# A hand-ordered pipeline for linear attention followed by a token and channel MLP: the next batch's attention between MLP matmuls, full 512-token groups, crossbar turns

## The chip, the cores and the metric

The kernel runs on one core of one Trainium2 chip. A core has a matmul engine (PE), which reads weights and moving operands from the on-chip buffer (SBUF) and writes accumulators (PSUM); a vector engine (DVE), a scalar engine (ACT) and a general engine (POOL); a queue engine (SyncE, SP in the profile); and 16 DMA engines that all queues share. Each engine runs its own instructions in order and waits on semaphores for the others.

The metric is the device time of one execution in microseconds. Every run is timed beside runs of the kernel before on the same chip. A ratio in this document is the mean time of one kernel's fast runs over the mean time of the other's fast runs of the same rounds, so it is not quite the ratio of the medians that stand beside it. A profile shows the span from the first to the last instruction, which is 1.7 to 1.9 us shorter than the time where both are on record for one execution.

## The reference, cut to what matters

```python
# q, k, v: 8 batches, 8 heads, 576 tokens, 64 channels, float32
def phi(x, c, s):                       # c, s: cos and sin of the token's position
    r = np.maximum(x, 0.0)
    return np.concatenate([r * c, r * s], axis=-1)        # 128 features
kv  = einsum('bhsf,bhsd->bhfd', phi(k), v);   z = phi(k).sum(tokens)
num = einsum('bhsf,bhfd->bhsd', phi(q), kv)
den = einsum('bhsf,bhf->bhs',  phi(q), z) + 1e-06
x   = (num / den) as [batch, 576 tokens, 512 channels]

h   = relu(x.T @ w_tok1) @ w_tok2       # mixes tokens: 576 -> 256 -> 576
u   = x + h.T
out = u + relu(u @ w_ch1) @ w_ch2       # mixes channels: 512 -> 1536 -> 512
```

About four fifths of the arithmetic, counted from these shapes, is in the last line, the channel MLP. Each batch's channel MLP needs its u, and u needs the batch's attention and both token products first. Batches do not depend on each other.

## The kernel before

It handles one batch after another; a scheduler orders each engine's instructions. 576 tokens are four tiles of 128 and one of 64. In this document, to *turn* a tile is to transpose it, to *evict* is to copy a finished result from PSUM to SBUF, *features* are the products phi(q) and phi(k), and *token-1* and *token-2* are the products with `w_tok1` and `w_tok2`. `uT` is the turned u, the input of the channel MLP.

```python
    for b in range(B):
        for ci, (o, sz) in enumerate(s_sizes):                # 128, 128, 128, 128, 64 tokens
            nc.sync.dma_start(out=qt[:sz], in_=q[b, :, o:o + sz, :].rearrange("h s d -> s h d"))
            nc.sync.dma_start(out=kt[:sz], in_=k[b, :, o:o + sz, :].rearrange("h s d -> s h d"))
            nc.gpsimd.dma_start(out=vt[:sz], in_=v[b, ...])   # cast to bf16 on the way
            # ... features: relu(q)*cos and *sin on ACT, relu(k)*cos and *sin on DVE ...
            for h in range(H):
                nc.tensor.matmul(kv_ps[:F, h * D:(h + 1) * D], kph, vt[:sz, h, :], ...)
                nc.tensor.matmul(z_ps[:F, h:h + 1], kph, ones[:sz, :], ...)      # one column
            for g in range(2):                                # turn the q features on PE
                for hh in range(HH):
                    nc.tensor.transpose(tr_ps[:F, hh, :sz], qph, ident[:sz, :sz])
                nc.scalar.copy(qpT[...], tr_ps[:F, :, :sz])
        # ... kv and z to SBUF ...
        for ci, (o, sz) in enumerate(s_sizes):
            for h in range(H):
                nc.tensor.matmul(num_ps[:sz, h * D:(h + 1) * D], lw, kv_sb[...], ...)
                nc.tensor.matmul(den_ps[:sz, h:h + 1], lw, z_sb[:F, h:h + 1], ...)
            # ... x_sb = num / den on DVE ...
        # ... b1_ps: 2 x 5 matmuls with w_tok1, relu on ACT; u_ps: 5 x 2 with w_tok2; u = u_ps + x ...
        for ci, (o, sz) in enumerate(s_sizes):                # turn u on PE, in float32
            for cj in range(NCC):
                nc.tensor.transpose(t_ps[...], u_sb[...], ident_f[:sz, :sz])
            nc.scalar.copy(uT[:, :, o:o + sz], t_ps[:, :, :sz])
        for mi in range(NCH):                                 # 12 slices of 128 hidden channels
            for (no, nsz) in [(0, 512), (512, 64)]:
                for ki in range(NCC):
                    nc.tensor.matmul(c_ps[:, no:no + nsz], w_ch1[...], uT[:, ki, no:no + nsz], ...)
            # ... relu to h1T, on ACT and DVE in turn ...
        for ci, (o, sz) in enumerate(s_sizes):                # five outputs, the last of 64 tokens
            for ki in range(NCH):
                nc.tensor.matmul(o_ps[:sz, :], h1T[:, ki, o:o + sz], w_ch2[:, ki, :], ...)
            # ... add u, store ...
```

## Time and profile before

| | kernel before |
|---|---|
| time, median of 2 runs | 418.03 us (417.87 to 418.19) |
| span of the profile | 415.3 us |
| first channel-MLP matmul | 69.2 us |
| one batch: channel MLP / the rest | about 25.2 / about 20.5 us |
| busy: PE, DVE, ACT, POOL | 85%, 39%, 39%, 15% |

The page of the profiled execution gives, for each engine, the busy time, its share of the span and the number of instructions; then slices of the span with the busy tenths; then shares of the chain that ended last.

```profile
span 415.3 us, 7475 instructions
...
PE 352.4 (85%) x3168; PEld 201.4 (48%) x3168; DVE 161.3 (39%) x332; ACT 162.6 (39%) x283; POOL 62.7 (15%) x72
...
PEclk9999559998799989998999979998999899998999
DMA  9999983029901393029702791029402900110002
...
PE 76%; DMA 7%; SPq 6%; DVE 5%; ACT 5%; issue 1%; DVEq 0%; ACTq 0%
...
```

PE is busy 85% of the span, yet its clock as granted by the throttle (PEclk, tenths) keeps dropping, and the DMA engines are at eight or nine tenths for the first six slices. Where does PE's time go? The windows view of two stretches, first one batch without its channel MLP and then its channel MLP, answers. Its columns are the stretch, its length, busy time and instruction count of PE, of PE's weight loads, of DVE, ACT and POOL, the granted clock, the DMA share and GB/s.

```profile
...
140.70:161.00 20.30, 18.47 (x242) 12.56 (x242) 12.75 (x31) 16.00 (x29) 6.72 (x5) 0.92 1.11 154
161.00:186.00 25.00, 25.00 (x156) 11.99 (x154) 7.31 (x10) 4.01 (x7) 0.00 (x0) 1.00 0.12 43
...
```

In the first of these two, attention and token mixing, PE counts as busy for 18.5 of 20.3 us at clock 0.92. The timeline of that stretch shows what this busy time is (start, length, engine, line, operation, shapes, count; in brackets the idle time before and what ended it).

```profile
...
146.94 0.24 PE L156 MATMUL den_ps<-z_sb,qpT 128*128 128x1 bf16 x4 [0.53 <-DVE den_sb L159]
...
150.42 3.41 PE L171 MATMUL b_ps<-x_sb,w_tok_118 128*128 128x512 bf16 x10
153.76 1.23 PE L133 MATMUL z_ps<-ones,kp 128*128 128x1 bf16 x40
...
157.73 2.82 PE L187 MATMUL t_ps<-ident_f,u_sb 128*128 128x128 f32 x20
160.88 0.38 PE L197 MATMUL c_ps<-uT,w_ch_127 128*128 128x512 bf16 x1 [0.33 <-ACT uT L189]
```

Ten token-1 matmuls take 3.41 us here, against 12 matmuls of the same width in 2.59 us in the MLP (216 ns each). The attention stretch of the batch before, 94 to 115 us, has a mean clock of 0.84. PE also waits for DVE or ACT several times, for 0.3 to 0.5 us each. Then 40 one-column z matmuls (1.2 us) and 20 turns of u in float32 (2.8 us) stand in the chain. Nothing of the next batch's MLP can fill these gaps, because its u does not exist yet.

### The profile page before, as it was taken

The numbers are of one execution on the slowest core, as the hardware profiler recorded it, in microseconds if no ns is written. First come the engines' busy times: TensorE is split into PE (matmuls) and PEld (weight loads), VectorE is DVE, ScalarE is ACT, GpSimd is POOL, SyncE is SP. The second block draws the span as 40 slices with busy tenths as digits, with TensorE's granted clock in tenths as the row PEclk, the third lists the DMA queues.
The fourth block names the chain that finished last, engine by engine and source line by source line (L and its number), as shares of the span: only waits on it lengthen the run. The fifth ranks groups of instructions, "written<-read, shape, count | busy, mean of one in ns | idle before, by whom it ended". The sixth has DMA issues, their size and how long they took to land.

```text
span 415.3 us, 7475 instructions
## 1 busy us (share of the span) xinstructions
PE 352.4 (85%) x3168; PEld 201.4 (48%) x3168; DVE 161.3 (39%) x332; ACT 162.6 (39%) x283; POOL 62.7 (15%) x72
## 2 busy tenths in 40 slices
PE   0005178998999999998999899998999899999996
PEld 0004154547454555447554655456554755465542
DVE  2002253327422554328332653346332743326231
ACT  4115164208531384209630664128520873051410
POOL 7363000006000320006000600024000600000000
PEclk9999559998799989998999979998999899998999
DMA  9999983029901393029702791029402900110002
GB/s 183 205 192 182 169 151 77 2 86 156 161 2 42 98 187 76 0 103 169 130 2 76 137 165 25 25 91 196 91 0 86 85 5 0 52 65 0 2 25 90
DMA packets 121043, 37.26 MB, mean 90 GB/s; under 512 B 113521, under 2 KB 115889, under 8 KB 121009
## 3 DMA queue, kind: packets, MB, share of 16 engines
q1 hardware_dynamic: 80256, 28.32, 30.7%
q0 software_dynamic: 40752, 8.46, 23.0%
q8 instruction: 25, 0.41, 0.5%
q14 instruction: 10, 0.07, 0.1%
HBM read 35.78 MB, written 9.44 MB: 109 GB/s over the span
## 4 chain that ended last, share of the span: by engine, by line
PE 76%; DMA 7%; SPq 6%; DVE 5%; ACT 5%; issue 1%; DVEq 0%; ACTq 0%
PE c_ps L197 23%; DMA kt<-in_k_dram 7%; PE b_ps L171 6%; PE num_ps L154 4%; PE tr_ps L141 4%; PE u_ps L179 4%; ACT uT L189 3%; SPq L113 3%; PE kv_ps L131 3%; SPq L112 3%; PE t_ps L187 3%; PE den_ps L156 2%; PE z_ps L133 2%; DVE kp L124 2%; DVE u_sb L181 1%; DVE kp L122 1%
## 5 line engine op out<-in xcount | busy, mean ns | idle before, releaser
L197 PE MATMUL c_ps<-uT,w_ch_127 128*128 128x512 bf16 (+1 forms) x768 | 97.0, 286 | 2.6 <-ACT uT L189 2.6
L114 POOL DMA_DIRECT2D vt<-in_v_dram x40 | 49.2, 1242 | 257.1 <-PE tr_ps L141 247.3
L142 ACT COPY qpT<-tr_ps 128x512 bf16<-128x512 bf16 (+1 forms) x80 | 40.4, 544 | 111.8 <-PE tr_ps L141 111.1
L197 PEld LDWEIGHTS <-w_ch_127 128*128 128x128 bf16 x768 | 51.0, 97 | 48.8 <-issue 2.5
L210 PEld LDWEIGHTS <-h1T 128*128 128x128 bf16 (+1 forms) x480 | 46.9, 100 | 55.3 <-issue 3.4
L205 DVE TENSOR_SCALAR h1T<-c_ps 128x576 bf16<-128x576 f32 x48 | 36.4, 758 | 83.2 <-PE c_ps L197 83.2
L203 ACT ACTIVATE h1T<-c_ps 128x576 bf16<-128x576 f32 x48 | 31.2, 650 | 61.4 <-PE c_ps L197 60.4
L120 ACT ACTIVATE qp<-qt,bias_112,cos_t 128x512 bf16<-128x512 f32 (+1 forms) x40 | 32.2, 805 | 23.1 <-DMA qt<-in_q_dram 23.1
L133 PE MATMUL z_ps<-ones,kp 128*128 128x1 bf16 (+1 forms) x320 | 10.5, 164 | 34.5 <-DVE kp L124 28.1
L181 DVE TENSOR_TENSOR u_sb<-u_ps,x_sb 128x512 f32<-128x512 f32 (+1 forms) x40 | 24.6, 681 | 30.0 <-PE u_ps L179 30.0
L122 DVE TENSOR_SCALAR kp<-kt,cos_t 128x512 bf16<-128x512 f32 (+1 forms) x40 | 19.9, 498 | 39.9 <-DMA kt<-in_k_dram 35.6
L156 PE MATMUL den_ps<-z_sb,qpT 128*128 128x1 bf16 (+1 forms) x320 | 18.5, 169 | 18.0 <-DVE den_sb L159 15.8
L121 ACT ACTIVATE qp<-qt,bias_112,sin_t 128x512 bf16<-128x512 f32 (+1 forms) x40 | 32.2, 804 | 1.7 <-DMA qt<-in_q_dram 1.7
L141 PE MATMUL tr_ps<-ident,qp 128*128 128x128 bf16 (+1 forms) x320 | 30.4, 221 | 0.7
L189 ACT CAST uT<-t_ps 128x512 bf16<-128x512 f32 (+1 forms) x40 | 20.1, 548 | 21.1 <-PE t_ps L187 20.1
L133 PEld LDWEIGHTS <-kp 128*128 128x128 bf16 (+1 forms) x320 | 9.4, 96 | 37.8 <-DVE kp L124 28.4
L164 DVE TENSOR_TENSOR x_sb<-num_ps,den_sb 128x512 bf16<-128x512 f32 (+1 forms) x40 | 25.3, 683 | 5.6 <-PE num_ps L154 4.9
L171 PE MATMUL b_ps<-x_sb,w_tok_118 128*128 128x512 bf16 (+1 forms) x80 | 26.7, 486 | 0.0
L156 PEld LDWEIGHTS <-qpT 128*128 128x128 bf16 (+1 forms) x320 | 16.0, 104 | 21.1 <-issue 17.9
L124 DVE TENSOR_SCALAR kp<-kt,sin_t 128x512 bf16<-128x512 f32 (+1 forms) x40 | 21.4, 535 | 3.3 <-DMA kt<-in_k_dram 3.3
L187 PE MATMUL t_ps<-ident_f,u_sb 128*128 128x128 f32 (+1 forms) x160 | 21.8, 273 | 0.9
L141 PEld LDWEIGHTS <-qp 128*128 128x128 bf16 (+1 forms) x320 | 20.8, 100 | 3.3 <-issue 0.2
(127 smaller groups left out, 307.3 us busy)
## 6 DMA issues: line engine op xcount, KB each, us to landing
qt<-in_q_dram SPq DMA_DIRECT2D x32, 256.0 KB, 6.5
kt<-in_k_dram SPq DMA_DIRECT2D x32, 256.0 KB, 5.5
out_dram<-res SPq DMA_DIRECT2D x32, 256.0 KB, 2.0
vt<-in_v_dram POOLq DMA_DIRECT2D x32, 128.0 KB, 6.9
w_ch_127<-in_moe_w_ch_dram POOLq DMA_DIRECT2D x4, 384.0 KB, 10.0
w_ch_132<-in_moe_w_ch_dram POOLq DMA_DIRECT2D x12, 128.0 KB, 8.4
qt<-in_q_dram SPq DMA_DIRECT2D x8, 128.0 KB, 3.9
kt<-in_k_dram SPq DMA_DIRECT2D x8, 128.0 KB, 3.5
```

What stands on the lines that cost most here:

```text
L114: nc.gpsimd.dma_start(out=vt[:sz], in_=v[b, :, o:o + sz, :].rearrange("h s d -> s h d"))
L120: nc.scalar.activation(qp[:sz, :, 0, :], qt[:sz], AF.Relu, bias=bias0[:sz], scale=c_s)
L121: nc.scalar.activation(qp[:sz, :, 1, :], qt[:sz], AF.Relu, bias=bias0[:sz], scale=s_s)
L141: nc.tensor.transpose(tr_ps[:F, hh, :sz], qph, ident[:sz, :sz])
L142: nc.scalar.copy(qpT[:F, g * HH:(g + 1) * HH, o:o + sz], tr_ps[:F, :, :sz])
L156: nc.tensor.matmul(den_ps[:sz, h:h + 1], lw, z_sb[:F, h:h + 1], start=True, stop=True)
L171: nc.tensor.matmul(b1_ps, w_tok1[:sz, ci, mi * P:(mi + 1) * P], x_sb[:sz, ci, :], start=(ci == 0), stop=(ci == NSC - 1))
L187: nc.tensor.transpose(t_ps[:P, cj, :sz], u_sb[:sz, ci, cj * P:(cj + 1) * P], ident_f[:sz, :sz])
L189: nc.scalar.copy(uT[:, :, o:o + sz], t_ps[:, :, :sz])
L197: nc.tensor.matmul(c_ps[:, no:no + nsz], w_ch1[:, ki, mi * P:(mi + 1) * P], uT[:, ki, no:no + nsz], start=(ki == 0), stop=(ki == NCC - 1))
L205: nc.vector.tensor_relu(h1T[:, mi, :], c_ps)
L210: nc.tensor.matmul(o_ps[:sz, :], h1T[:, ki, o:o + sz], w_ch2[:, ki, :], start=(ki == 0), stop=(ki == NCH - 1))
```

## The change

The intent: PE should never run attention alone. Every instruction is placed by hand. While PE does the channel MLP of group g, the attention steps of batch g+1 are put between its matmuls, one small step after every four MLP matmuls, and the features of batch g+2 are computed on ACT, DVE and POOL. Further parts of the same change:

- Each batch's MLP takes 512 of its 576 tokens; the eight tails of 64 tokens form a ninth group at the end, so every MLP matmul has 512 columns.
- z and den become a 65th column of the kv and num matmuls.
- The q features and u are turned by crossbar DMA transposes from the SyncE queue instead of on PE. Only the first batches' turns stay on PE.
- Tokens are dealt to partitions so that four or five neighbouring tokens are contiguous in HBM: packets of 1 to 1.25 KB instead of 256 bytes, two loads per tensor and batch.

```diff
-    for b in range(B):
-        ... loads, features, kv, z, turns, num, den, token mixing, turns, MLP of batch b ...
+    ctx.enter_context(tc.manual_schedule())
+    ... batch 0 up to its uT, and the features and q turns of batch 1 ...
+    for g in range(B + 1):                       # nine groups; the last holds the tails
+        b = g + 1                                # attention of this batch now
+        f = g + 2                                # features of this one
+        if g + 3 < B:
+            loads(g + 3, (nc.sync, nc.sync))
+        for s in range(24):
+            if s < 12: ps = mlp1(g, s)           # four matmuls of 512 columns
+            else:      mlp2(g, t, part, mps[t])  # four matmuls of 512 columns
+            if b < B:
+                if s < 5:          kv(b, s);  if s == 4: kv_out(b, ACT)
+                elif 6 <= s < 11:  num(b, s - 6); x_out(b, s - 6)
+                elif s in (12, 13): b1(b, s - 12); b1_out(b, s - 12, ACT)
+                elif s in (15, 16):
+                    u_mm(b, s - 15); u_out(b, s - 15)
+                    u_cast(b, s - 15, ACT); uturn_dma(b, s - 15)
+                elif s == 17 and b % 2: tail_mm(b); tail_out(b)
+            ... evict mlp1 or mlp2 of this step ...
+            if f < B:
+                if 7 <= s < 12:    kfeat(f, s - 7, DVE, ACT); vcast(f, s - 7, POOL)
+                if 13 <= s < 23 and s % 2 == 1:
+                    qfeat(f, j, DVE, ACT); qturn_dma(f, j)
 ... (cut: helpers, the new layout of weights and tokens, the start)
+    def uturn_dma(b, c):
+        nc.sync.dma_start_transpose(out=uT[b % 2][...], in_=u_bf[...])     # 256 KB
+    def qturn_dma(b, j):
+        nc.sync.dma_start_transpose(out=qpT[:, :, j, :], in_=qp[j]...)     # 256 KB
```

(Engine names are written out here; `s`, `j`, `t` and `part` are counters. The part before the loop is the *start* in what follows, and the change from one group to the next is a *boundary*.)

## The prediction

> **What bounds it now.** The chain of waits gives PE 76% of the 415.3 us span. The timeline splits it: first channel-MLP matmul at 69.2 us; then each batch takes 45 to 46.5 us: about 25.2 of channel MLP at granted clock 1.00, and about 20.5 of attention and token mixing, where PE counts as busy but is held by hand-offs (windows: clock 0.84 to 0.92). 69 + 8×25.2 + 7×20.5 ≈ 414. ACT, DVE and POOL are busy 39%, 39% and 15%. The first 55 us are DMA-bound (DMA share 9 tenths).
>
> **What the change does.**
> 1. MLP: 40 token tiles, 8 of them half empty, plus 64-column matmuls become nine full groups of 96 matmuls of 512 columns. Twelve took 2.59 us, 216 ns each: 20.7 us a group, 186 instead of 201 us in all. Gain about 15 us.
> 2. Attention of the next batch goes between MLP matmuls. Its PE work: 40 kv and 40 num matmuls (eight 64-column ones took about 0.25 us, so 1.3 us each set), ten token-1 matmuls 2.2, eight token-2 ones 1.7, tails 0.4; z and den vanish into a 65th column, turns leave PE. About 6.8 us a batch instead of 20.5; a group with attention is 27.5 us of PE. Main gain: about 7×13 us, all on the critical path.
> 3. ACT per group, from trace durations: eight evictions 4.8, ten features at 0.80, B1 1.2, casts about 2.4: 17 us. DVE: five x outputs at 1.05, two u adds about 1.35 each, four evictions, four results, ten features at 0.48: 18 us. Both fit under PE; DVE lags by about 1.5 us in the num steps.
> 4. Turns: seven 256 KB crossbar DMAs a group; no trace here has one. The Trainium skill, "DMA: Bandwidth & Descriptors", "Latency and other measured facts", gives 261 GB/s for a non-contiguous DMA transpose; estimate from it: 1 us plus 2 us latency. The chain from the last token-2 matmul: u add 1.4, queueing and cast 1.5, turn 3: about 6 us, against seven MLP steps of 0.86 = 6.0. It just fits; I allow 1.5 us a group of bubble.
> 5. Loads: 256-byte packets (80256 hardware packets averaged 25 ns of an engine) become 1 KB or more. Estimate: a group's 3.5 MB in 12 us, below the period. Start: 7.1 MB of inputs (batch 1's features stand before batch 0's u on DVE and ACT) plus 7.5 MB of weights, about 44 us, then 11 us of chain: first MLP at about 56 us instead of 69.
>
> **Sum.** 56 + 7×29 + 2×20.7 + 3 (last result and store) = 303 us span, plus 2.7 as now: about 306 us. Range 286 to 348. Chances: faster by over 2% 0.96, within 2% 0.02, slower 0.02.
>
> **What would show each step.** Timeline: last two groups 20.7 us, first seven about 29; first mlp1 matmul near 56 us. Groups: 864 MLP matmuls, no z or den. Waits: a group's first mlp1 matmul waits 0 to 3 us for uT; num waits little. Issues: turns landing in 2.5 to 4 us. PE share of the chain over 85%; clock near 1.00 from 60 us on.
>
> **What would make it wrong.** Slow turns: seven in one queue in order, at over 4 us each they exceed the 28 us period and every group stretches (at 6 us: +13 us a group, about 400 us). Weights starving the input queues (start at 65 us or more). DVE backlog or PSUM recycling stalling PE (group 32: 327 us). POOL casts slowing DVE. Faster: no bubble and a start at 48 us: about 288 us.

## The result, and the profile after

| | before | after | predicted |
|---|---|---|---|
| time, median of 2 runs | 418.03 us | 326.5 us (325.71 to 327.3) | 306 us (286 to 348) |
| ratio of the fast runs | | 0.7805, 95% interval 0.7754 to 0.7856 | |
| span | 415.3 us | 323.8 us | 303 us |
| first channel-MLP matmul | 69.2 us | 65.4 us | 56 us |
| the seven groups with attention, mean | | 30.4 us | 29 us |
| the last two groups | | 20.7 and 20.9 us | 20.7 us |
| end, after the last group | | 4.1 us | 3 us |

The page after, the same lines as before:

```profile
span 323.8 us, 4680 instructions
...
PE 264.1 (82%) x1760; PEld 132.2 (41%) x1760; DVE 154.4 (48%) x320; ACT 132.0 (41%) x205; POOL 42.4 (13%) x76
...
PEclk9999999999999997999999979999999999999999
DMA  7999999700299749955995899278019502501102
...
PE 54%; DMA 20%; DVE 16%; ACT 4%; issue 3%; SPq 1%; ACTq 1%; DVEq 0%
...
```

PE's busy share even fell a little, from 85% to 82%: a busy share says little about whether the time is well spent. What changed is the busy time itself, from 352.4 to 264.1 us, and the clock line, which is full in all but two slices. The windows view, one stretch for each group (the same columns as above), gives the sum:

```profile
...
65.41:95.70 30.29, 28.23 (x201) 13.80 (x199) 18.71 (x37) 16.06 (x25) 4.66 (x6) 1.00 0.29 63
95.70:125.39 29.69, 27.38 (x195) 13.54 (x196) 16.67 (x35) 14.74 (x23) 3.06 (x5) 1.00 0.84 218
125.39:157.37 31.98, 29.86 (x198) 14.58 (x199) 18.02 (x36) 15.36 (x24) 4.66 (x6) 0.95 0.82 204
...
188.07:220.11 32.04, 29.62 (x198) 14.46 (x199) 18.02 (x36) 15.36 (x24) 4.66 (x6) 0.95 0.76 204
...
278.07:298.80 20.73, 20.73 (x97) 9.42 (x97) 5.53 (x8) 4.67 (x8) 0.00 (x0) 1.00 0.14 54
...
```

Groups are alternately with and without a tail step, 28.2 and 27.4 us of PE work at full clock. The groups from 125.39 and from 188.07 show clock 0.95, and there the PE busy time is longer by 1.4 to 1.6 us for the same instructions. What stands between the PE work and the group's length is shown by the waits of PE (who waited, for whom, us in total, times, the longest):

```profile
...
PE psM L291 <- DMA uT<-u_bf: 13.1, 6, 3.0
...
```

and by the timeline at two boundaries:

```profile
...
125.39 1.20 PE L291 MATMUL psM<-uT,w_ch 128*128 128x512 bf16 x4 [2.03 <-DMA uT<-u_bf]
...
126.83 1.90 PE L291 MATMUL psM<-uT,w_ch 128*128 128x512 bf16 x4
...
```

```profile
...
95.70 1.04 PE L291 MATMUL psM<-uT,w_ch 128*128 128x512 bf16 x4 [1.79 <-DMA uT<-u_bf]
...
96.82 1.03 PE L291 MATMUL psM<-uT,w_ch 128*128 128x512 bf16 x4
...
```

Both boundaries begin with a wait of about 2 us for the turned u. After the first of them four MLP matmuls take 1.90 us, against 1.03 us after the second: the clock had been lowered. The windows view of the 4.1 us from 125.39 gives a granted clock of 0.59:

```profile
...
125.39:129.50 4.11, 4.11 (x26) 2.13 (x27) 0.00 (x0) 1.19 (x2) 0.81 (x2) 0.59 1.40 242
...
```

In finer windows it is 0.50 for 3.4 us, from about 126.1 to 129.5 us, and 1.00 on both sides. The length of the wait alone does not decide this: the boundaries at 220.11 and 249.96 us waited 2.15 and 2.21 us and kept the full clock.

The turn itself: the queue of SyncE at one boundary (SPq is issue time in the queue, before the data moves), and the list of DMA issues with the median time to landing.

```profile
...
87.70 1.23 SPq L249 DMA_TRANSPOSE uT<-u_bf  x1
89.10 1.23 SPq L153 DMA_TRANSPOSE qpT<-qp  x1
90.42 1.36 SPq L249 DMA_TRANSPOSE uT<-u_bf  x1
91.87 1.70 SPq L279 DMA_TRANSPOSE uTt<-u_bt  x1
93.74 2.71 SPq L153 DMA_TRANSPOSE qpT<-qp  x2
```

```profile
...
uT<-u_bf SPq DMA_TRANSPOSE x14, 4.0
...
```

The second u turn was issued at 90.42 us, although its input was ready at 89.40 us, since the q turn ahead of it held the queue for 1.23 us. It landed 5.2 us later, at 95.6 us, while a tail turn and further q turns followed it into the same DMA engines. The first u turn of the same boundary, issued into an empty queue at 87.70 us, landed after 2.7 us. At 278.07 us, the one boundary without q turns, PE does not wait for uT at all.

The start is told by the chain of waits in order of time (start, length, what), from the landing of batch 1's q at 42.3 us to the first MLP matmul at 65.4 us:

```profile
...
20.60 21.69 DMA q_raw<-in_q_dram
...
47.40 0.61 ACT qp L131
48.01 0.49 ACT B L222
...
52.99 1.24 DVE u_sb L239
...
55.35 1.04 PE psA L257 x8
...
58.13 1.24 DVE u_sb L239
...
60.49 1.03 PE psA L257 x8
...
64.42 1.16 PE psA L160 x16
65.57 0.86 PE psM L291 x4
...
```

The inputs of two batches had landed by 42.3 us, close to the 44 us of the prediction. The chain behind took 23 us, not 11: 5.6 us of batch 1's features on ACT, ahead of batch 0's first B1 eviction; then two token-1 products, each waiting for an eviction; then the two halves of u one wholly after the other, 10 us; then the 40 q turns of batch 1 (psA L160) in front of the first MLP matmul, 4 us.

Order is not all of it: PE runs at about half pace in this stretch. Five token-1 matmuls take 2.30 us at 48.54 us and 1.08 us in a group (81.61 us); eight turns take 1.04 us here and 0.61 us in the groups of u_on_pe. Summed over the token-1, token-2 and u-turn matmuls of this stretch, that is about 4 of the 23 us. The clock column shows 1.00 here all the same, so in the start it is not borne out by the durations; whether the throttle is the reason is not shown.

### The profile page after: what moved, and what is told of

The parts are those of the page before. It is cut to its first block, busy times and chain, and to the rows that moved or that the text cites. A ratio compares the mean times of both kernels' runs of the same rounds, so it can differ in the third digit from the quotient of the medians.

```text
span 323.8 us, 4680 instructions
## 1 busy us (share of the span) xinstructions
PE 264.1 (82%) x1760; PEld 132.2 (41%) x1760; DVE 154.4 (48%) x320; ACT 132.0 (41%) x205; POOL 42.4 (13%) x76
## 4 chain that ended last, share of the span: by engine, by line
PE 54%; DMA 20%; DVE 16%; ACT 4%; issue 3%; SPq 1%; ACTq 1%; DVEq 0%
PE psM L291 22%; PE psM L303 17%; DMA uT<-u_bf 9%; DMA q_raw<-in_q_dram 7%; PE psA L234 5%; PE psA L216 4%; DVE x_sb L206 4%; DMA v_raw<-in_v_dram 4%; PE psA L174 3%; DVE kp L133 3%; DVE rden L203 2%; DVE u_sb L239 2%; DVE x_tl L206 1%; SPq L124 1%; DVE rden L202 1%
## 5 line engine op out<-in xcount | busy, mean ns | idle before, releaser
L291 PE MATMUL psM<-uT,w_ch 128*128 128x512 bf16 x384 | 98.1, 386 | 13.1 <-DMA uT<-u_bf 13.1
L303 PE MATMUL psM<-w_ch,h1T 128*128 128x512 bf16 x432 | 99.9, 379 | 0.0
L297 ACT ACTIVATE h1T<-psM 128x512 bf16<-128x512 f32 x72 | 42.8, 597 | 80.5 <-PE psM L291 76.7
L303 PEld LDWEIGHTS <-h1T 128*128 128x128 bf16 x432 | 42.2, 98 | 53.6 <-issue 3.3
L291 PEld LDWEIGHTS <-w_ch 128*128 128x128 bf16 x432 | 37.3, 98 | 50.1 <-issue 9.5
L299 DVE TENSOR_SCALAR h1T<-psM 128x512 bf16<-128x512 f32 x36 | 24.8, 688 | 68.2 <-PE psM L291 68.2
L150 POOL CAST vb<-v_raw 128x512 bf16<-128x512 f32 x35 | 22.2, 645 | 148.7 <-PE psA L174 93.8
L308 DVE TENSOR_TENSOR res<-psM,u_sb 128x512 f32<-128x512 f32 x32 | 22.1, 689 | 34.0 <-PE psM L303 34.0
L131 ACT ACTIVATE qp<-q_raw,sin_t 128x512 bf16<-128x512 f32 x40 | 27.2, 713 | 17.9 <-DMA q_raw<-in_q_dram 12.1
L244 ACT CAST u_bf<-u_sb 128x1024 bf16<-128x1024 f32 x16 | 16.7, 1045 | 27.3 <-DVE u_sb L239 21.6
L131 ACT ACTIVATE kp<-k_raw,sin_t 128x512 bf16<-128x512 f32 x40 | 27.1, 711 | 1.9 <-DMA k_raw<-in_k_dram 1.9
L216 PE MATMUL psA<-x_sb,w_tok 128*128 128x512 bf16 x64 | 18.1, 409 | 10.4 <-ACT B L222 10.0
L194 PEld LDWEIGHTS <-qpT 128*128 128x128 bf16 x320 | 15.8, 102 | 10.4 <-issue 2.1
## 6 DMA issues: line engine op xcount, KB each, us to landing
w_ch<-in_moe_w_ch_dram POOLq DMA_DIRECT2D x4, 384.0 KB, 18.7
```

The costliest lines, as they stand in the source:

```text
L131: eng.activation(out_ap, in_ap, AF.Relu, bias=0.0, scale=s)
L194: nc.tensor.matmul(ps[:, h // HH, (h % HH) * E1:(h % HH + 1) * E1], qpT[:, h, j, :], kv_sb[:, h, 0:E1], start=True, stop=True, skip_group_ ...
L216: nc.tensor.matmul(ps[:, mi, :], w1[:, j, mi * P:(mi + 1) * P], rhs, start=(j == 0), stop=(j == NJ - 1))
L291: nc.tensor.matmul(ps.rearrange("p (t k) -> p t k", k=P), wc1[:, ki, mi * P:(mi + 1) * P], src[:, :, ki, :], start=(ki == 0), stop=(ki == ...
L297: eng.activation(h1T[:, mi, :], ps, AF.Relu)
L299: eng.tensor_relu(h1T[:, mi, :], ps)
```

## The experiments

All kernels differ from the changed kernel ("the control") by the edit shown. The control was run again in the last rounds. The ratios are to the kernel before in the same rounds.

| run | median us (fast runs) | ratio to before | ratio to before over the control's 0.7800 |
|---|---|---|---|
| again (control) | 324.99 | 0.7800 | 1 |
| not_between | 420.1 | 1.0055 | 1.289 |
| u_on_pe | 312.48 | 0.7490 | 0.960 |
| u_turn_first | 311.58 | 0.7457 | 0.956 |
| warm | 319.83 | 0.7663 | 0.982 |
| q_on_pe | 353.05 | 0.8460 | 1.085 |
| small_packets | 407.6 | 0.9771 | 1.253 |
| many_issues | 329.70 | 0.7955 | 1.020 |
| start (wrong result) | 328.06 | 0.7894 | 1.012 |
| start_u_on_pe (wrong result) | 316.91 | 0.7609 | 0.976 |
| start_fixed | 314.58 | 0.7556 | 0.969 |
| start_and_u_first | 299.91 | 0.7224 | 0.926 |

The 95% intervals of the ratios to before are at most 0.6 percentage points to either side. The last column is worked out from two ratios and carries both errors, and for all runs but many_issues, start_fixed and start_and_u_first it also compares across chips.

### 1. Is it the interleaving? (not_between)

```diff
-        for s in range(NS):
-            ... MLP step s; attention step s of batch b; features step s of batch g+2 ...
+        for step in range(2 * NS):
+            s = step % NS
+            ... step < NS:  MLP step s; features step s of batch g+1 (for g > 0)
+            ... step >= NS: attention step s of batch b, alone
```

The features had to move by one batch, because the attention that reads them now comes later than the features of the following batch would overwrite them; they stay hidden under the MLP.

> Undoes the interleaving alone: the kv, num, token-mixing and u steps of the next batch stand as one block after the MLP matmuls of the group; features, loads, merged z and den columns, nine groups and crossbar turns stay. Theory (the gain is mostly that attention's hand-offs hide behind MLP matmuls): a group grows from the 30.4 us of the changed kernel's timeline to 20.7 of MLP plus a block of about 23 us (kv 3, x outputs 6, two token-1 products and evictions 6, token-2 product, u adds, cast and turn 8), so 40 to 45 us; total 390 to 430 us, near the kernel before. Rival (the gain is fewer and fuller instructions, so the order matters little): a group near 31 us, total near 330 us.

Measured: 420.1 us (418.7 to 421.39), ratio 1.0055 to the kernel before. In the profile, a group takes 43.8 to 44.3 us (group starts at 105.34, 149.13, 193.41 and 237.71 us). The timeline of one block:

```profile
...
85.03 1.38 PE L174 MATMUL psA<-vb,kp 128*128 128x65 bf16 x40
...
90.44 0.60 PE L194 MATMUL psA<-kv_sb,qpT 128*128 128x65 bf16 x8 [0.62 <-DVE x_sb L206]
...
95.49 1.50 PE L216 MATMUL psA<-x_sb,w_tok 128*128 128x512 bf16 x4 [0.69 <-ACT B L222]
...
105.34 1.03 PE L291 MATMUL psM<-uT,w_ch 128*128 128x512 bf16 x2 [4.31 <-DMA uT<-u_bf]
```

and the windows view of the MLP before the next block and of that block:

```profile
...
105.34:128.00 22.66, 22.66 (x95) 9.83 (x96) 8.79 (x17) 10.77 (x18) 0.00 (x0) 0.89 0.77 214
128.00:149.13 21.13, 10.31 (x101) 5.30 (x99) 7.98 (x18) 3.89 (x5) 2.85 (x5) 0.80 0.35 80
...
```

The interval of the ratio just excludes 1 and everything is within 2%: with the order taken away, nothing of the 91 us gain is left. The block is again a chain of hand-offs, about 21 us, as long as in the kernel before, although z, den and all steady turns have left PE and its busy time in the block fell from 18.5 to between 10 and 12 us. Two things make it so. The wait for the crossbar turn of u is 4.2 to 5.7 us a group, where PE's own u turns and their eviction took about 3.2 us; and the rest of the chain is only about 1 us shorter (15 to 17.4 us against 17 to 18). The MLP after a block also runs at a clock of 0.88 to 0.89, which costs about 2 us a group. This does not show that the other parts are worth nothing inside the pipeline, where PE's work does set the time of a group; the old work in the new order was not run.

### 2. What makes the stall at the boundary? (u_turn_first, u_on_pe)

The first run changes only the order of the SyncE queue:

```diff
                     qfeat(f, j, V, A)
-                    qturn_dma(f, j)
+                    if j == 0: qturn_dma(f, 0)
+                    elif j == 2: qturn_dma(f, 1); qturn_dma(f, 2)     # behind both u turns
+                    elif j > 2: qturn_dma(f, j)
```

> Only the order in the SyncE queue changes: the second q turn is issued after both u turns instead of between them. Theory A (queueing: the u turn waits about 1 us for the q turn ahead of it): the second u turn is issued and lands about 1 us earlier, the PE wait for uT falls by about 1 us a boundary, total about 318 us. Theory B (the turn's own time to landing of 4 to 5 us under other traffic is the cause): the issue comes earlier but the landing hardly moves, total 324 to 328 us.

Measured: 311.58 us (310.38 to 311.68). The queue and PE's wait for uT:

```profile
...
87.23 2.95 SPq L249 DMA_TRANSPOSE uT<-u_bf  x2
90.27 1.24 SPq L279 DMA_TRANSPOSE uTt<-u_bt  x1
91.61 4.39 SPq L153 DMA_TRANSPOSE qpT<-qp  x3
```

```profile
...
PE psM L291 <- DMA uT<-u_bf: 2.6, 2, 1.9
...
```

The order in the queue is the cause, as theory A said, but the gain is about twice what it said, and its reason was only half of it. The two u turns now leave back to back (2.95 us for both), so the second is issued some 1.0 us earlier. It also lands sooner: at the first boundary 2.7 us after its issue, against 5.2 us before. The median over all u turns fell from 4.0 to 3.1 us, and the wait from 13.1 us to 2.6 us. So the time to landing that theory B named was part of the stall, and it depends on the order too. Fewer turns ahead of it and beside it fit this; which of them counts was not measured. All seven groups show clock 1.00: their sum is 199.2 us instead of 212.7 us. Of these 13.4 us, 10.5 us are the wait itself and about 3 us the lowered clock after it. Two waits are left in this run, 1.9 and 0.7 us, and the clock stayed full after them.

The second run takes the u turns to PE, where 16 transposes and two copies on DVE replace them:

```diff
                     u_cast(b, s - 15, A)
-                    uturn_dma(b, s - 15)
+                elif s in (19, 21):
+                    uturn_pe(b, (s - 19) // 2, V)
```

> The u turns of the steady groups go to PE (16 transposes and two DVE copies a batch) in place of the crossbar DMA; q turns stay on the crossbar. Theory (the stall at each group boundary is the u turn's DMA, and the low clock after two of the boundaries follows from that stall): PE's wait for uT falls from 13 us in all to under 2, the clock stays at 1.00 in all groups, PE work grows by 0.9 us a batch; groups from 30.4 to about 28.6 us, total about 312 us. Rival (the stall is DVE and ACT running late with the u add and cast): the wait stays at 1.5 us or more a boundary and the total rises to 328 to 333 us.

Measured: 312.48 us (312.2 to 313.61). PE's waits for uT are gone, the clock is 1.00 in every group, and groups take 28.4 and 29.2 us (without and with a tail step). The rival, that DVE and ACT deliver u too late, falls: they deliver u at the same time here. The PE price of the turns is 0.7 us of busy time a group, a little under the 0.9 us expected. The narrow spread of the four times, 1.4 us against 3.8 us for the control, fits: without a stall no boundary draws the low clock.

### 3. Is the clock after a stall a cost of its own? (warm)

```diff
         mps = {}
+        if 0 < g < B - 1:
+            fill = nextA()
+            for i in range(8):          # results that nobody reads
+                nc.tensor.matmul(fill[:, 0, :], ident, wc2[:, i, :], start=True, stop=True, ...)
```

> Eight matmuls of 512 columns whose result nobody reads are put at the boundaries, 1.7 us of PE work where PE otherwise waits for uT. Theory (after a stall over about 2 us the clock falls to 0.6 for some 4 us and costs up to 2 us): groups that had clock 0.95 show 1.00, total 1 to 4 us lower, 322 to 325 us. Rival (the slow matmuls after the stall wait for data): clock and first matmul times unchanged, total the same or up to 3 us higher.

Measured: 319.83 us (318.92 to 321.0), about 5 us under the control. A group of this run, in the windows view, that stands where the first profile had clock 0.95 (125.39):

```profile
...
122.96:154.00 31.04, 29.96 (x206) 14.68 (x206) 18.02 (x36) 15.36 (x24) 4.68 (x6) 1.00 0.84 211
...
```

No group shows a clock under 1.00, in spite of waits of up to 1.3 us that remain. The fills and the waits that remain together take as long as the waits did in the control (about 13 us), so the stalls have not become shorter; they are filled. So matmuls that compute nothing made the kernel faster. The seven groups together took 209.3 us, 3.3 us less than in the control's profile; another 2.4 us of the difference between these two profiles lies in the start (62.1 against 64.5 us), which the edit does not touch, so that part is spread between executions (profiles with this same start have it at 62.1 to 65.4 us). The direction is shown, and the size of about 3 us agrees with what the control lost in its two slow groups (1.6 and 1.5 us). The threshold in the expectation, a stall over about 2 us, is not shown: a stall of 3.15 us in the control kept the full clock, one of 2.03 us in the first profile did not. Which boundary is hit changes from run to run: in the first profile the groups from the second and fourth boundary were slow, in the control's the second and the sixth.

### 4. Is the late start DMA or order? (start, start_u_on_pe, start_fixed)

```diff
-    for j in range(NJ): kfeat(1, j, V, A); vcast(1, j, G); qfeat(1, j, V, A)
     for mi in range(NT): b1(0, mi); b1_out(0, mi, A)
     for c in range(2):
         u_mm(0, c); u_out(0, c); u_cast(0, c, A)
+    for c in range(2):
         uturn_pe(0, c, V)
-    for j in range(NJ): qturn_pe(1, j, (V, A)[j % 2])
+    for j in range(NJ): kfeat(1, j, V, A); vcast(1, j, G)
 ... group 0, steps 0 to 5:
+            if g == 0 and s < NJ: qfeat(1, s, V, A)
+            if g == 0 and 1 <= s < NJ + 1: qturn_pe(1, s - 1, (V, A)[s % 2], nextM())
```

> Only the order before and in the first group changes: batch 0's B1, u and its turns come before batch 1's features, both token-2 products before the first turn, and batch 1's q features and turns move into the first six steps of group 0. Theory (the late start, 65.4 us against the 56 predicted, is the in-order chain after the inputs have landed at 42.4 us, not the DMA itself): the first MLP matmul comes at 46 to 52 us, total about 310 to 314 us. Rival (the DMA is the limit, weights and inputs landing until about 42 us and later): the first matmul may come earlier, but the first group stretches by as much waiting for wc2 or batch 1's inputs, total 322 to 328 us.

This version gave a wrong result (relative error 0.12), by a mistake in the edit: the loads of batch 3, which overwrite batch 1's inputs, still stood ahead of batch 1's q features, so these read batch 3's q and also waited for it. The first MLP matmul came at 47.5 us, but group 0 took 50 us and the time was 328.06 us. The same mistake sat in a run with the u turns on PE as well:

> Both edits together: the reordered start and the u turns on PE. If the two causes are separate, the gains add: about 16 us from the start and 12 to 14 us from the boundaries, total 294 to 300 us. If the early start only moves the wait into the first groups, the total stays above 308 us.

It took 316.91 us and, being wrong too, decides nothing. The mended edit issues those loads five steps later:

```diff
-        if g + 3 < B: loads(g + 3, ...)
+        if 0 < g and g + 3 < B: loads(g + 3, ...)
         for s in range(NS):
+            if g == 0 and s == NJ: loads(3, ...)
```

> The reordered start, with its fault mended: batch 3's loads, which overwrite batch 1's inputs, are issued after batch 1's q features have read them. Theory (the late start is the in-order chain after the inputs have landed): first MLP matmul at about 47.5 us as in the faulty run, first group 28 to 34 us, total 307 to 314 us. Rival (the DMA is the limit): the first group stretches to 40 us or more, total above 320 us.

Measured: correct, 314.58 us (312.1 to 316.18), 10.4 us under the control, a little outside the expected range of the theory and under the rival's. The first MLP matmul:

```profile
...
47.85 1.54 PE L291 MATMUL psM<-uT,w_ch 128*128 128x512 bf16 x4 [0.78 <-DVE uT L262]
...
```

It comes at 47.85 us instead of 64.5, and the first group takes 34.6 us instead of 30.3. So the earlier start is worth 16.7 us, of which 4.4 us go back into a first group that now has the 40 q turns of batch 1 in it and starts at a low clock. No wait for weights or inputs on PE appears in this group. So the 23 us behind the landing were order, and the half pace that went with it, not DMA. The 42 us up to the landing are untouched by this edit.

### 5. Would PE have been the better place for the q turns? (q_on_pe)

```diff
                     qfeat(f, j, V, A)
-                    qturn_dma(f, j)
+                if 14 <= s < 24 and s % 2 == 0:
+                    qturn_pe(f, (s - 14) // 2, ...)
```

> The q turns of the steady groups go to PE (40 transposes of about 55 ns, so 2.2 us, and five copies of 0.7 to 1.0 us on DVE and ACT a batch) and the u turns stay on the crossbar. Theory (each turn alone lands in 3 to 4 us; the q turns around it delay the u turn): PE work a group 29.7 to 30.4 us, the boundary wait shrinks to under 1 us, groups 30.5 to 31 us, total 326 to 331 us, about even. If the q turns did no harm to u, the boundary wait stays near 2 us and the total is 337 to 342 us.

Measured: 353.05 us (349.49 to 354.31), worse than both guesses. The u turn, alone in the queue now, landed after 2.7 us (median) and PE never waited for it. A new wait took its place:

```profile
...
PE psA L160 <- ACT qp L131: 29.2, 21, 2.9
...
```

A turn on PE stands in PE's own order, one step behind a feature that ACT computes, and ACT at that point is behind the store of a result that PE itself has to finish first. 29.2 us in 21 waits are spent so, of which 5.0 us in 3 waits lie in the start, where the control has them too. The crossbar turn costs no PE order: if it is late, only its reader waits. The run shows that this placement is bad, not that any placement on PE would be; the u turns of experiment 2, put four and five steps behind their cast, had no wait at all.

### 6. Are the larger packets needed? (small_packets, many_issues)

```diff
-            got.append(eng.dma_start(out=dst[par:P:2, :, at:at + hi - lo, :], in_=s[:, :, lo:hi, :]))
+            for n in range(lo, hi):            # small_packets: one load a token, 256 bytes
+                eng.dma_start(out=dst[par:P:2, :, at + n - lo, :], in_=s[:, :, n, :])
+            for h in range(0, H, 2):           # many_issues: one load for two heads, 1 KB and more
+                eng.dma_start(out=dst[par:P:2, h:h + 2, at:...], in_=s[:, h:h + 2, lo:hi, :])
```

> One load for each token of nine instead of two per tensor and batch: the same bytes in 256-byte packets instead of 1 to 1.25 KB, and 27 issues a batch instead of six. Theory (larger packets matter for the start and leave room in the steady groups): batch 1's q lands at 55 to 65 us instead of 42.4, the first MLP matmul comes 13 to 22 us later, and the groups stretch because 3.5 MB at about 161 GB/s take 22 us of each 30 beside the turns on the same queue; total 345 to 380 us. Rival (packet size is hidden): the start moves by less than 5 us and the total stays under 333 us.

> Each load is cut into four by heads: packets stay at 1 to 1.25 KB, but a batch takes 24 issues instead of six, as the small-packet run took 27. It tells the two sides of that run apart. If the packet size made its start late and the number of issues stretched its groups: here the first MLP matmul comes at 62 to 68 us, and PE waits for uT at the boundaries 8 to 14 us each, total 370 to 395 us. If the packet size did both: start and boundaries as in the changed kernel, total 323 to 332 us.

Measured: 407.6 us (405.1 to 408.07) with small packets, 329.70 us (329.58 to 333.63) in the three fast executions with many issues of full packets. The first MLP matmul came at 77.1 us with small packets. The fourth many-issues execution, 336.29 us, was slow, and it is the one profiled, so its stretches are not used. By the time of the fast ones, the number of issues alone costs about 2%, not the 45 to 70 us expected of it: that side of the second expectation fell, and the side "packet size did both" is the nearer one.

The small-packet run does not measure a DMA rate, though. In its groups PE waits 72 us in all for uT, because the SyncE queue, in which the turns stand behind the loads, was itself stuck:

```profile
...
SPq L125 <- DMA out_dram<-res: 76.7, 10, 27.5
...
```

Its loads waited 76.7 us for result stores. Why a load waits for a store is not shown; that the two came to share a completion semaphore when 27 loads a batch were dealt out is a guess, and many_issues, with 24 loads a batch, has no such wait in its profile. Of the 83 us over the control, about 13 us lie in the start (77.1 against 64.5 us) and 59 us in longer waits for uT (72.3 against 12.9 us). How much of this is slow packets and how much is queues stuck behind each other is open.

### 7. The two findings together (start_and_u_first, again)

> The changed kernel as it is, a control on the chip of the other three runs. Its first two runs were 325.71 and 327.3 us; expected 322 to 329 us. Its profile should again show PE waiting for uT at six boundaries, 1.5 to 3 us each; which boundaries show the low clock may differ.

> The mended start and the q turn moved behind both u turns. If start and boundary are separate causes the gains add: 12 to 18 us from the start, 13 to 15 us from the boundaries, total 293 to 300 us, the fastest of all. If they overlap, 302 to 310 us.

Measured: 324.99 us (322.17 to 325.92) for the control and 299.91 us (298.92 to 302.39) for the mended start with the q turn moved behind both u turns. It is correct and the fastest of all, ratio 0.7224 to the kernel before and 0.926 to the control. The gains add: 10.4 us of start and 13 to 15 us of boundary (the control's median, or the changed kernel's own first one, less 311.58) make 24 to 25, and 25.1 us were measured.

The page of that run, busy time and clock:

```profile
...
PE 258.5 (87%) x1760; PEld 130.1 (44%) x1760; DVE 153.4 (52%) x319; ACT 132.5 (45%) x206; POOL 42.4 (14%) x76
...
PEclk9999995999999999999999999999999999999999
...
```

PE is busy 87% of the span, against 82% in the first profile after the change, with the same 1,760 matmuls, and the clock is full in every slice but the one around the first MLP matmul.

## Why the prediction was right, and where it was off

The range held and the mechanism held. The size was off by 20.5 us (326.5 against 306), and all its parts err to the late side, so no error hid another. The spans say where: start 9.4 us, seven groups 9.7 us (212.7 against 203), end 1.1 us, last groups 0.2 us.

1. **Nine full groups.** Predicted 20.7 us a group; the last two took 20.7 and 20.9 us. Right.
2. **Attention between MLP matmuls as the main gain.** Shown by not_between: without it the whole gain is gone. The PE work of a group, 27.5 us predicted, was 27.4 us without a tail and 28.2 us with one. Right. The prediction put the gain down to 20.5 us becoming 6.8 us of PE work, as if z, den and turns leaving PE were part of it; not_between shows that these do next to nothing for a chain that PE runs alone. It also took the 20.5 us for hand-offs only; part of them was PE at half clock.
3. **DVE and ACT fit.** Predicted 18 and 17 us a group, the windows show 16.7 to 18.7 and 14.7 to 16.1. The lag of DVE behind the num steps was real and cost PE 0.3 us a group. Right.
4. **The bubble of 1.5 us a group.** This term was mis-sized. The chain from the last token-2 matmul to the landing was put at 6 us; at the first boundary it took 8.6 us (87.0 to 95.6). The u add and the cast were right (1.2 and 1.0 us). The turn was put at 3 us: 1 us from the 261 GB/s of the Trainium skill's page "DMA: Bandwidth & Descriptors" and 2 us of latency. That fits a turn issued into an empty queue (2.7 us), but the one that the boundary waits for took 5.2 us, and about 1 us more passed in the queue, behind a q turn. Measured: landing 4.0 us in the median over all u turns, a wait of 1.8 to 3.0 us at each of six boundaries, and 1.4 and 1.6 us of lowered clock after two of them. Together 2.5 us a group over the PE work.
5. **The start at 56 us.** The landing was right (42.3 against 44 us), the chain behind it was mis-sized: 23 us measured, 11 us estimated. The estimate summed the work of each engine and let the engines overlap. The order of each engine forbade it: ACT had ten features ahead of the eviction on which the chain hung, and PE had a turn of the first half of u ahead of the matmuls of the second. PE's half pace, about 4 us, was not in the estimate either. start_fixed gave back 16.7 us of the chain at the first matmul.
6. **A marker that failed.** The prediction said PE's share of the chain of waits would rise over 85%. It fell from 76% to 54%, while DMA rose from 7% to 20% and DVE from 5% to 16%. The DMA part is in good part the turn of u (9%), the bubble of point 4. The DVE part is another matter: in the num steps PE waits 0.3 us for DVE once, and the chain, followed back from there, runs through DVE for several microseconds in which PE was busy all the same. A share of the chain is not a share of a bottleneck where two engines are both nearly full.

A second marker, a clock near 1.00 from 60 us on, failed at two boundaries. The prediction does not say on what rate its 12 us for a group's loads and its 44 us for the start rest.

What is open: the rate of small packets inside the pipeline (6), what the merged columns, full groups and crossbar turns are worth within the new order, why a turn lands later beside others, and the exact condition under which the clock falls after a stall.

## What to carry to other kernels

When a stage is a chain of hand-offs between engines, taking work out of it may not shorten it at all; putting another batch's dense matmuls around it hides it whole. Here, taking that order back cost all of the 91 us gained. After such a change look at the two places where the pipeline has nothing to hide behind: the fill at the start, where each engine's order decides which chain can overlap, and the boundary, where one transfer that the next group needs should be first in its queue. Estimate a latency that sits on a boundary with its queue and its neighbours in it, not from a bandwidth.

## What the Trainium skill lacked or had wrong

- "DMA: Bandwidth & Descriptors", "Latency and other measured facts", gives a bandwidth for the DMA transpose, 261 GB/s. That section has no time for which one holds its issuing queue, nor one to landing. (The page's part on trn3 B0 has cycle counts of an issue, also for earlier generations, without the size of a tile.) Here a turn of 128 x 1024 bf16 within SBUF (256 KB) held the SyncE queue for 1.23 to 2.09 us (1.28 us in the median) and landed after 4.0 us in the median (2.7 to 5.6 us), so about 66 GB/s end to end (256 KB over 4.0 us); with fewer turns beside it, 2.7 us in the median (q_on_pe).
- "TensorE: Matmul & The Clock Gate", "HAM oscillation — how this bites in real kernels", states the rule as "no PE-idle gaps >~3.4µs". Here the granted clock fell to 0.50 for about 3.4 us after PE waits of 2.03 us (first profile), 2.11 and 2.21 us (control), and not after one of 3.15 us (control). That the window is free-running, as the same page says, fits the boundary changing from run to run; the figure 3.4 us as a safe length does not hold in this case. The page advises to avoid gaps and, for benchmarks, to warm up first; that eight useless matmuls at each boundary inside a kernel keep the clock up and pay for themselves (about 3 us in all, warm) it does not say.
- The section "Why this matters for your kernels" of the same page asks to keep PE busy; no page says that turns placed on PE bind PE's order to the engine that makes their input (q_on_pe: 29.2 us in 21 waits, 5.0 us of them in the start).
